# Batch 1's softmax divided behind v, the float64 shift on another engine, pinned first conversions and halved k loads in a fused attention and mixer kernel

## The chip, the cores and the metric

The kernel runs on one core of a Trainium2 chip. A core has a matrix engine (TensorE, PE in the rows, with its weight loads as PEld), a vector engine (VectorE, DVE), an engine for activation functions (ScalarE, ACT), a general one (GpSimd, POOL), an engine whose sequencer starts transfers here (SyncE, SP), and 16 DMA engines. Each engine runs its instructions in one fixed order, and semaphores make one wait for another. Data lie in SBUF (128 partitions), sums of matmuls in the banks of PSUM. The metric is the device time of one execution in microseconds; before the change it is 533.94 us, the median of three runs (531.52 to 535.51).

## What is computed

Four batches of 576 positions, 8 heads of 64. Heads 0 to 3 look at the last 32 positions, heads 4 to 7 at every 32nd. The weights of the mixers come as float64.

```python
scores = np.where(mask, q @ k.T / np.sqrt(64), -1e9)
attn = np.exp(scores - scores.max(-1))
x = (attn / (attn.sum(-1) + 1e-9)) @ v            # heads side by side: [4, 576, 512]
h = np.maximum(x @ w_in, 0)                       # first mixer
u, v = h[..., :512], h[..., 512:]
vn = (v - v.mean(-1)) / np.sqrt(v.var(-1) + 1e-6)
x = (u * (w_spatial @ vn + b_spatial)) @ w_out
th = x @ w_theta                                  # second mixer
u = x + w_tok_r @ (x * cos(th)) + w_tok_i @ (x * sin(th))
out = u + np.maximum(u @ w_ch, 0)
```

## The kernel before

All products of the mixers are made from float16 halves: a number is split into a high and a low half, and three matmuls (high by high, low by high, high by low) are added in PSUM. A weight arrives as raw float64 in a staging tile (`x2f`, `zf`, `xT`, before these are needed for themselves) and is put together as float32 by `from_f64` (line 200): ScalarE scales the upper words (L207), VectorE shifts the lower words (L208) and joins them (L209, L210); `part` then makes the halves, the high one on ScalarE (L119), the low one on GpSimd (L215). There are 15 such conversions: four of w_in, two each of w_out, w_theta and w_ch, five of the token weights.

Attention runs over 11 units a batch (`units`, line 274); a unit is two blocks of 96 or 128 queries with 128 keys for two heads, four softmax tiles. Batches 0 and 1 use `attention32` (line 420) in float32, batches 2 and 3 `attention` (line 488) in float16 halves. A unit of `attention32` goes through TensorE's mask matmuls and scores (`scores32`, L398, L403), VectorE's maximum (L410), ScalarE's four exponentials with their sums (L420) and two small instructions (L418, L354), VectorE's reciprocal and division (L357, L358), TensorE's four transposes (L460), ScalarE's copy of them (L461), the product with v (L435), and the eviction into xT, the high half by ScalarE (L370), the low one by VectorE (L371). In batch 1, transposes and products share one PSUM bank, `av`, of which there is one; scores have another, `sc`. k comes with zeros beside it (`padded`), so that one matmul of 128 partitions sees one head.

A batch of the mixers is `main_v` (v, its normalisation `rstd` and vn), `main_mid` (u and sp chunks, then x, then th with the sines of z, stored transposed by DMA into `zf`) and `main_end` (y over the token weights, then c and the store). Their evictions have a raised priority (`hv`, `ha`, `hg`).

The program is written in one order and the scheduler puts each engine's instructions in order by priorities and readiness as it estimates them. `ATT_AT` says at which count of matmul columns the steps of the next batch's attention are written into the mixers, `CONV_SP` to `CONV_CH` the same for the conversions, `WIN_AT` after which steps of batch 0's attention the four w_in conversions are written. So batch 0's attention comes first with w_in's conversions in it, then batch 0's v, then `main_mid(0)` with batch 1's attention in it; what is left of that is drained, then `main_v(1)`, then `main_end(0)` with batch 2's attention.

Of the kernel before, what the change touches and what calls it, by code (L numbers as in the profile page):

```python
# [15 lines left out]
I64 = mybir.dt.int64  # L16
AF = mybir.ActivationFunctionType
# [17 lines left out]
E_WAY = ('aaaadaaadaa', 'aaaaaaaaaaa')  # L35
# [19 lines left out]
WIN_AT = (0, 0, 0, 0, 1, 0, 1, 0)  # L55
# [9 lines left out]
def kernel(  # L65
# [31 lines left out]
    NZ = 2 * S // P  # L97

# [35 lines left out]
    nc.gpsimd.tensor_copy(identb, ident)  # L134
    halfpi = const.tile([P, 1], F32, name="halfpi")
# [64 lines left out]
    def from_f64(stg, x, n):  # L200
# [6 lines left out]
        nc.scalar.activation(hi.bitcast(F32), hi.bitcast(F32), AF.Copy, scale=F64_SHIFT)  # L207
        nc.vector.tensor_scalar(xi, lo, 29, None, op0=ALU.logical_shift_right)  # L208
# [11 lines left out]
    def prep_w(dst, src, c, i, late=True):  # L220
        stg, x = stage(raw2)
        n = c.stop - c.start
        nc.sync.dma_start(pair(stg, n), src[i * P:(i + 2) * P, c].rearrange("(a p) n -> p a n", p=P))
        x = pair(from_f64(stg, x, 2 * n), n)
# [62 lines left out]
    def prep_qk(b, hp, j, tiles):  # L287
        local = hp < 2
        nk = S + STRIDE if local else S
        if j == 0:  # L290
            qT = att_p.tile([P, 2, S], F16, tag="qT", name="qT", bufs=2)
            kT = att_p.tile([P, 2, 2, S + STRIDE], F16, tag="kT", name="kT", bufs=2)
# [21 lines left out]
    def load32(b, hp):  # L314
# [3 lines left out]
        kv = att_p.tile([P, 2, S + STRIDE], F32, tag="kT", name="k32", bufs=2)  # L318
# [10 lines left out]
        vv = att_p.tile([P, 6, 2, 64], F32, tag="vT", name="v32", bufs=2)  # L329
        nc.sync.dma_start(vv[:, 0:nb], vl_d[b, hp] if local else vs_d[b, hp - 2])  # L330
# [8 lines left out]
    def softmax_exp(u, sc, sm, st):  # L339
# [83 lines left out]
    def attention32(b):  # L423
# [5 lines left out]
        for s in range(NU + 2):  # L429
# [483 lines left out]
```

## Time and profile before

| | us |
|---|---|
| median of 3 runs | 533.94 |
| the profiled execution | 533.31 |
| its span in the trace | 531.5 |
| TensorE busy in the span | 481.9 |
| VectorE busy | 357.2 |
| ScalarE busy | 309.8 |
| GpSimd busy | 92.8 |

In the profile a row of a timeline is start in us, duration in us, engine, line, operation, tiles (out<-in), shapes and count, and in brackets how long the engine was idle ahead of it and what released it. A table by stretches gives the stretch and its length, then for each of PE, PEld, DVE, ACT and POOL the busy time and the count, TensorE's granted clock as a share of 2.4 GHz, the DMA engines' busy share and GB/s. A group by line gives its count, then busy us and mean ns, then the idle time ahead with what ended it. A wait row gives the instruction, what it waited for, the total in us, the times and the longest. The stretches used are: 0 to 56.56 batch 0's attention (in it most of v's first matmuls), to 63.70 the rest of its v, to 155.21 u, sp, x and th of batch 0 with batch 1's attention, to 169.85 batch 1's v, to 203.18 batch 0's y, and then all the rest.

### The profile page before, as it was taken

To read this page: it belongs to the slowest core of one execution; us is meant where nothing else is said; L and a number is where in the kernel's file an instruction comes from. 1 tells how busy PE (TensorE), PEld (TensorE's weight loads), DVE (VectorE), ACT (ScalarE), POOL (GpSimd) and SP (SyncE) were. 2 spreads that over 40 slices of the span, in tenths; PEclk is the share of its full clock that TensorE was granted. 3 is DMA by queue.
4 is the path that set the end of the run, shared out by engine and by line. 5 is a ranking of instruction groups with operands and counts; after the bars stand their busy time and mean duration, and the time that the engine had idled before them with its cause. 6 is when DMAs were issued, how large, how long until landed. Compare 5 with 4: busy or idle time off the path is not lost. (4 is left out here: it accounts for less than half of the span.)

```text
span 531.5 us, 10195 instructions
## 1 busy us (share of the span) xinstructions
PE 481.9 (91%) x4019; PEld 362.3 (68%) x4019; DVE 357.2 (67%) x721; ACT 309.8 (58%) x751; POOL 92.8 (17%) x58
## 2 busy tenths in 40 slices
PE   5577976889798979999899998999999999998996
PEld 5564554667564757777675886777757777776774
DVE  1789789899959988888649877875289221226512
ACT  2787767678799246786676456865593111238202
POOL 0021115463300261001000400000001400100110
PEclk9789989999999989999999999999999999999999
DMA  8875652844339404666419035532054011002702
GB/s 273 316 242 176 211 197 77 267 123 172 122 72 190 157 5 119 189 131 154 123 37 166 1 58 138 153 53 41 1 110 69 1 46 46 1 1 51 129 2 89
DMA packets 75700, 59.88 MB, mean 113 GB/s; under 512 B 59778, under 2 KB 60802, under 8 KB 75652
## 3 DMA queue, kind: packets, MB, share of 16 engines
q1 hardware_dynamic: 75652, 59.23, 41.7%
q8 instruction: 31, 0.51, 0.4%
q14 instruction: 17, 0.14, 0.1%
HBM read 40.08 MB, written 4.72 MB: 84 GB/s over the span
## 5 line engine op out<-in xcount | busy, mean ns | idle before, releaser
L532 PE MATMUL y<-wtok,zf 128*128 128x288 f16 x864 | 108.5, 288 | 1.5 <-DMA zf<-vn 1.5
L532 PEld LDWEIGHTS <-zf 128*128 128x128 f16 x864 | 84.6, 99 | 24.5 <-DMA zf<-vn 1.8
L532 PE MATMUL sp<-wsp,vn 128*128 128x288 f16 x384 | 50.5, 286 | 3.8 <-ACT vn L108 1.9
L532 PE MATMUL c<-x2h,wch 128*128 128x288 f16 x384 | 48.8, 286 | 2.4 <-ACT o L108 2.4
L532 PE MATMUL u<-xT,win 128*128 128x288 f16 x384 | 50.5, 290 | 0.0
L532 PEld LDWEIGHTS <-vn 128*128 128x128 f16 x416 | 40.3, 98 | 14.3 <-ACT vn L108 2.1
L532 PE MATMUL th<-x2h,wth 128*128 128x288 f16 x384 | 49.7, 290 | 0.0
L532 PE MATMUL x<-zf,wout 128*128 128x288 f16 x384 | 49.2, 286 | 0.0
L108 POOL TENSOR_TENSOR x2h<-x2f,x2h 128x576 f16<-128x576 f32 x20 | 27.0, 1349 | 109.9 <-DVE x2h L108 47.6
L532 PEld LDWEIGHTS <-wch 128*128 128x128 f16 x384 | 37.3, 98 | 12.1 <-issue 3.0
L592 PE MATMUL v<-win,xT 128*128 128x512 f16 x192 | 43.5, 379 | 1.6 <-ACT xT L370 1.4
L532 PEld LDWEIGHTS <-wth 128*128 128x128 f16 x384 | 37.7, 99 | 10.3 <-issue 0.5
L532 PEld LDWEIGHTS <-win 128*128 128x128 f16 x384 | 37.9, 99 | 9.7
L532 PEld LDWEIGHTS <-wout 128*128 128x128 f16 x384 | 37.1, 98 | 9.4
L348 ACT ACTIVATE sm<-sm,st 96x128 f32<-96x128 f32 (+1 forms) x88 | 34.2, 390 | 8.1 <-DVE st L344 8.1
L592 PEld LDWEIGHTS <-xT 128*128 128x128 f16 x192 | 18.3, 98 | 23.5 <-ACT xT L370 2.3
L108 POOL TENSOR_TENSOR zf<-u,zf 128x576 f16<-128x576 f32 x8 | 14.0, 1746 | 112.1 <-ACT zf L108 112.1
L108 ACT ACTIVATE x2h<-x2f 128x576 f16<-128x576 f32 x24 | 16.4, 685 | 28.8 <-DVE x2f L108 28.4
L358 DVE TENSOR_TENSOR sm<-sm,st 96x512 f32<-96x512 f32 (+1 forms) x33 | 29.6, 897 | 0.9
L108 DVE SCALAR_TENSOR_TENSOR x2f<-y,x2f 128x576 f32<-128x576 f32 x16 | 12.0, 753 | 26.5 <-PE y L532 26.4
L108 DVE TENSOR_TENSOR ta<-ta,x2f 128x1152 f32<-128x1152 f32 x16 | 21.6, 1353 | 9.7 <-ACT ta L108 9.7
L108 ACT ACTIVATE o<-c 128x576 f32<-128x576 f32 (+1 forms) x17 | 10.3, 613 | 29.9 <-PE c L532 29.7
(132 smaller groups left out, 861.5 us busy)
## 6 DMA issues: line engine op xcount, KB each, us to landing
qs<-in_qd_dram SPq DMA_DIRECT2D x16, 288.0 KB, 2.8
out_dram<-o SPq DMA_DIRECT2D x15, 288.0 KB, 2.1
ks<-in_kl_dram SPq DMA_DIRECT2D x8, 304.0 KB, 3.2
k<-in_kzs_dram SPq DMA_DIRECT2D x4, 576.0 KB, 6.1
ks<-in_ks_dram SPq DMA_DIRECT2D x8, 288.0 KB, 3.0
x2f<-in_w_in_dram SPq DMA_DIRECT2D x2, 1024.0 KB, 5.2
zf<-in_w_in_dram SPq DMA_DIRECT2D x2, 1024.0 KB, 9.9
xT<-in_w_ch_dram SPq DMA_DIRECT2D x2, 1024.0 KB, 6.2
```

The source lines that it names most:

```text
L108: return f(*args, **kwargs)
L348: nc.scalar.activation(sm[0:R, n, :], sm[0:R, n, :], AF.Exp, bias=st[0:R, 1, n:n + 1], scale=-1.0, accum_out=st[0:R, 2, n:n + 1])
L358: N[eng].tensor_tensor(sm[0:R], sm[0:R], st[0:R, 3, :].unsqueeze(2).broadcast_to([R, 4, P]), ALU.mult)
L532: nc.tensor.matmul(ps, lhs, rhs, **kw)
L592: nc.tensor.matmul(ps, xh[:, xe, c, i * P:(i + 1) * P], win[:, we, c, DM:2 * DM], start=(c == 0 and n == 0), stop=(c == NC - 1 and n == 2))
```

## The change

1. The first two w_in loads are issued together, and their conversions keep the order of the program (`win_ahead`, `pin`); `WIN_AT` is moved.
2. The shift of the lower words in `from_f64` goes from VectorE to ScalarE, which reads one byte of each and scales it.
3. k of batches 0 and 1 is loaded in two halves of 64 partitions, without zeros, into two constant tiles `kts` zeroed once by VectorE; the first loads are issued by ScalarE's sequencer, and the mask comes in two halves. Batches 2 and 3 use the same two tiles for their k.
4. Batch 1 has a function of its own. Its mask is added by VectorE, which finds the maximum in the same instruction (the form of batches 2 and 3). v carries columns of ones, so its product brings the sums of the exponentials along; it is made with the probabilities as stationary operand, is divided as it leaves PSUM, and is transposed after that. The pipeline has one step more.

```diff
-WIN_AT = (0, 0, 0, 0, 1, 0, 1, 0)
+WIN_AT = (0, 1, 0, 0, 0, 1, 0, 1)
...
+    kts = [const.tile([P, 2, S + STRIDE], F32, name=f"kt{i}") for i in range(2)]
+    for t in kts:
+        nc.vector.memset(t[0:64, 1, :], 0.0)
+        nc.vector.memset(t[64:P, 0, :], 0.0)
...
-        nc.scalar.activation(hi.bitcast(F32), hi.bitcast(F32), AF.Copy, scale=F64_SHIFT)
-        nc.vector.tensor_scalar(xi, lo, 29, None, op0=ALU.logical_shift_right)
+        order = tc.keep_in_program_order if pin else lambda ins: ins
+        order(nc.scalar.activation(hi.bitcast(F32), hi.bitcast(F32), AF.Copy, scale=F64_SHIFT))
+
+        top = stg.bitcast(U8)[:, 0:8 * n].rearrange("p (n w) -> p n w", w=8)[:, :, 3]
+        order(nc.scalar.activation(xi, top, AF.Copy, bias=1.0 / 64 - 0.5, scale=1.0 / 32))
...
+    def win_ahead(half):
+        c = slice(half * DM, (half + 1) * DM)
+        loaded = {}
+
+        def load():
+            for i in range(0, NC, 2):
+                loaded[i] = load_w(w_in, c, i)
+
+        return [load] + [lambda i=i: prep_w(win, w_in, c, i, False, loaded[i]) for i in range(0, NC, 2)]
...
-            nc.sync.dma_start(kv[..., k0:k1], ksrc[..., k0:k1])
-            if first and i == 0:
-                nc.sync.dma_start(mask, mask_d)
-                nc.scalar.activation(maskb, mask, AF.Copy)
...
+            for j in range(2):
+                h = slice(64 * j, 64 * j + 64)
+                (nc.scalar if first else nc.sync).dma_start(kv[h, j, k0:k1], ksrc[h, j, k0:k1])
...
+            vv = att_p.tile([P, 6, VW], F32, tag="vT", name="v32", bufs=2)
+            nc.gpsimd.memset(vv[:, 0:nb, 0:VW:VW - 1], 1.0)
+            nc.sync.dma_start(vv[:, 0:nb, 1:VW - 1], vsrc.rearrange("p n j d -> p n (j d)"))
...
+    def attention1(b):
...
+            if s >= 3:
+                xn, rows = xs.pop(s - 3)
+                for i, hp, blk, r0, R, o, t0 in pv_blocks(s - 3):
+                    nc.tensor.transpose(xt[:, o:o + R], xn[0:R, i, :], ident[0:R, 0:R])
+            if 2 <= s < NU + 2:
+                sm, pT, st, xn = un.pop(s - 2)
+                for i, hp, blk, r0, R, o, t0 in pv_blocks(s - 2):
+                    for j in range(2):
+                        c = slice(j * (VW // 2), (j + 1) * (VW // 2))
+                        nc.tensor.matmul(pv[0:R, i, c], pT[:, 2 * i + j, r0:r0 + R], tabs[hp][2][:, blk, c],
+                                         start=True, stop=True)
+                ri = st[0:R, 3, :].rearrange("p (i j) -> p i j", i=2)
+                nc.scalar.activation(ri, pv[0:R, :, 0:VW:VW - 1], AF.Copy, bias=1e-9 / XS, scale=1.0 / XS)
+                nc.vector.reciprocal(st[0:R, 3, :], st[0:R, 3, :])
+                nc.vector.tensor_tensor(xn[0:R].rearrange("p i (j d) -> p i j d", j=2),
+                                        pv[0:R, :, 1:VW - 1].rearrange("p i (j d) -> p i j d", j=2),
+                                        ri.unsqueeze(3).broadcast_to([R, 2, 2, 64]), ALU.mult)
+                xs[s - 2] = xn, R
+            if s >= 3:
+                x_evac(xT[b % 2], spans_of(s - 3), xt)
...
+                softmax_exp(s, [sc[:, n, :] for n in range(4)], sm, st, False)
```

In the changed kernel the lines are numbered anew: L216 and L219 are the scale and the shift of a conversion, L456 batch 0's exponentials and L384 those of the other batches, L492 and L406 batch 0's copy of transposes and the eviction's high half, L407 its low half; in batch 1 L547 are the transposes of the exponentials, L548 their copy, L516 the product with v, L519 to L521 the division, L510 the transposes behind it.

ScalarE early in batch 0's attention, before: `at` are scores, `smx` exponentials, `x2f` the first part of w_in.

```order
L418 ACTIVATE st_134<-st_134 96x4
L420 ACTIVATE smx_124,st_134<-at_125,st_134 96x128 x4
L418 ACTIVATE st_149<-st_149 96x4
L207 ACTIVATE x2f_99<-x2f_99 128x1024
L420 ACTIVATE smx_141,st_149<-at_142,st_149 96x128 x4
L354 ACTIVATE st_134<-st_134 96x4
L418 ACTIVATE st_180<-st_180 96x4
```

The first conversion stands ahead of the second unit's exponentials. The same conversion in the changed kernel:

```order
L492 ACTIVATE smx_214<-sc_263 128x4x96
L216 ACTIVATE x2f_105<-x2f_105 128x1024
L219 ACTIVATE x2h_106<-x2f_105 128x1024
L406 ACTIVATE xT0_101<-av_275 128x192
L492 ACTIVATE smx_247<-sc_306 128x4x96
L456 ACTIVATE smx_319,st_327<-at_320,st_327 128x128 x3
L492 ACTIVATE smx_288<-sc_337 128x4x96
L216 ACTIVATE zf_104<-zf_104 128x1024
L121 ACTIVATE win_87<-x2h_106 128x2x512
```

It stood at row 6 of ScalarE's order and stands at row 34 now, behind the exponentials of the first units, and a shift follows it.

ScalarE where batch 0's th ends and batch 1's v begins, before: `ta` are the sines and cosines, `vn` here the halves of z, `xT1` batch 1's xT.

```order
L108 ACTIVATE vn_97<-ta1_1475 128x1152
L108 ACTIVATE ta3_1554<-ta3_1554 128x576
L370 ACTIVATE xT1_96<-av_1522 128x18x14
L108 ACTIVATE vn_97<-ta2_1511 128x1152
L108 ACTIVATE ta3_1554<-ta3_1554,halfpi_79 128x576
L108 ACTIVATE ta3_1554<-ta3_1554 128x576
L119 ACTIVATE kT_1849<-ks_1852 128x608
L119 ACTIVATE qT_1848<-qs_1924 128x576
L307 ACTIVATE vT_1999<-vs_1895 128x768
L108 ACTIVATE vn_97<-ta3_1554 128x1152
```

Batch 1's last eviction (L370) stands among the sines. In the changed kernel, at the same sines:

```order
L519 ACTIVATE st_1330<-av_1467 126x4
L216 ACTIVATE xT0_101<-xT0_101 128x1024
L110 ACTIVATE vn_103<-ta2_1546 128x1152
L110 ACTIVATE ta3_1594<-ta3_1594,halfpi_85 128x576
L110 ACTIVATE ta3_1594<-ta3_1594 128x576
L406 ACTIVATE xT1_102<-av_1467 128x18x4
L384 ACT_TABLE_LOAD
L384 ACTIVATE sm_1882,st_1883<-sm_1882,st_1883 96x128
L110 ACTIVATE vn_103<-ta3_1594 128x1152
L406 ACTIVATE xT1_102<-av_1467 128x18x4
```

The evictions here are those of the ninth unit of eleven; a shift, a table load and an exponential of batch 2 stand between.

TensorE where batch 1's last product with v stands, before:

```order
L532 LDWEIGHTS wth_85
L532 MATMUL th2_1486<-x2h_100,wth_85 128x288
L435 MATMUL av_1522<-pT32_1367,v32_1207 64x126 x4
L532 LDWEIGHTS wth_85
L532 MATMUL th3_1529<-x2h_100,wth_85 128x288
```

It stood in batch 0's th stage. In the changed kernel the last unit's transposes, products and transposes behind the division stand in batch 1's v stage, among scores of batch 2 (L560):

```order
L560 LDWEIGHTS qT_1774
L560 MATMUL sc_1948<-kt0_79,qT_1774 96x128
L547 MATMUL av_1481<-ident_70,sm_1399 128x128 x4
L510 MATMUL av_1557<-ident_70,pT32_1329 128x126 x2
L516 MATMUL av_1557<-v32_1235,pT32_1400 126x65 x4
L510 MATMUL av_1605<-ident_70,pT32_1400 128x126 x2
```

Behind it come one group of scores more and the last 39 of batch 1's 60 v matmuls; 21 stand ahead.

## Rows read from the trace of the kernel before

**Rows 1.** Table by stretches of the span: busy time of each engine.
```profile
0.00:18.80 18.80, 7.92 (x57) 7.21 (x58) 4.85 (x11) 6.38 (x23) 0.99 (x7) 0.89 0.88 306
18.80:39.81 21.01, 17.01 (x143) 14.76 (x143) 18.49 (x35) 18.10 (x72) 4.25 (x2) 0.85 0.74 250
39.81:56.56 16.75, 13.18 (x97) 7.19 (x95) 15.10 (x24) 12.81 (x42) 4.47 (x2) 1.00 0.57 188
...
63.70:155.21 91.51, 76.42 (x624) 58.47 (x624) 80.17 (x114) 68.13 (x178) 33.81 (x14) 0.96 0.47 154
155.21:169.85 14.64, 13.16 (x70) 5.63 (x68) 13.38 (x22) 14.61 (x24) 0.00 (x0) 1.00 0.83 146
169.85:203.18 33.33, 29.99 (x253) 23.69 (x253) 30.81 (x70) 16.01 (x36) 13.42 (x7) 0.95 0.31 88
203.18:531.50 328.32, 317.07 (x2751) 242.34 (x2749) 189.29 (x443) 168.13 (x373) 35.89 (x26) 1.00 0.34 77
```

**Rows 2.** Timeline, all engines: where the longest wait of TensorE ends.
```profile
16.23 1.14 ACT L207 ACTIVATE x2f<-x2f 128x1024 f32<-128x1024 f32 x1 [5.74 <-DMA x2f<-in_w_in_dram]
16.23 0.69 DVE L208 TENSOR_SCALAR x2h<-x2f 128x1024 int32<-128x1024 int32 x1 [5.98 <-DMA x2f<-in_w_in_dram]
...
18.80 0.58 PE L398 MATMUL at<-maskb,identb 128*96 128x256 bf16 x2 [5.92 <-ACT smx L420]
```

**Rows 3.** TensorE's waits, 0 to 70 us.
```profile
PE at L403 <- DMA k<-in_kzl_dram: 2.3, 2, 1.3
```

**Rows 4.** TensorE's waits, 65.15 to 155.21 us.
```profile
PE av L460 <- DVE xT L371: 9.5, 4, 3.5
...
PE av L460 <- DVE sm L358: 1.7, 3, 0.7
```

**Rows 5.** Groups by line, 65.15 to 155.21 us.
```profile
L358 DVE TENSOR_TENSOR sm<-sm,st 96x512 f32<-96x512 f32 (+1 forms) x10 | 13.8, 1378 | 0.2
...
L410 DVE TENSOR_REDUCE st<-sc 96x4 f32<-96x512 f32 (+1 forms) x10 | 6.7, 674 | 0.5 <-PE sc L403 0.4
...
L207 ACT ACTIVATE zf<-zf 128x1024 f32<-128x1024 f32 (+1 forms) x4 | 4.9, 1224 | 0.8 <-DMA zf<-in_w_tr_dram 0.5 <-DMA zf<-in_w_out_dram 0.3
...
L371 DVE TENSOR_TENSOR xT<-av,xT 128x192 f16<-128x192 f32 (+2 forms) x11 | 3.8, 342 | 0.5 <-ACT xT L370 0.4
L398 PE MATMUL sc<-maskb,identb 128*128 128x512 bf16 (+2 forms) x10 | 3.6, 376 | 0.0
```

**Rows 6.** Timeline, GpSimd and VectorE near 87 us.
```profile
85.72 4.32 POOL L108 TENSOR_TENSOR vn<-vr,vn 128x1024 f16<-128x1024 f32 x1 [1.25 <-ACT vn L108]
...
87.98 2.61 DVE L358 TENSOR_TENSOR sm<-sm,st 96x512 f32<-96x512 f32 x1
```

**Rows 7.** Timeline of TensorE: the v stages of batch 0 and batch 1.
```profile
55.69 0.60 PE L592 MATMUL v<-win,xT 128*128 128x512 f16 x2 [0.48 <-ACT xT L370]
...
162.94 6.22 PE L592 MATMUL v<-win,xT 128*128 128x512 f16 x28 [0.23 <-DVE xT L371]
```

**Rows 8.** Timeline of ScalarE: exponentials of the first unit.
```profile
7.88 0.36 ACT L420 ACTIVATE smx<-at,st 96x128 f32<-96x128 f32 x1
8.14 0.19 ACT L420 ACTIVATION_READ_ACCUMULATOR smx<-at,st 96x1 f32 x1
8.23 0.35 ACT L420 ACTIVATE smx<-at,st 96x128 f32<-96x128 f32 x1
```

**Rows 9.** Timeline of VectorE: the mask form that batches 2 and 3 use.
```profile
165.33 0.28 DVE L344 CUSTOM_DVE_ANT_0 sm<-sc,mask 96x128 f32<-96x128 f32 x1
...
165.54 0.28 DVE L344 CUSTOM_DVE_ANT_0 sm<-sc,mask 96x128 f32<-96x128 f32 x1
```

**Rows 10.** Timeline of TensorE in the y stage of batch 0.
```profile
187.95 4.57 PE L532 MATMUL y<-wtok,zf 128*128 128x288 f16 x36
195.86 1.01 PE L473 MATMUL sc<-kT,qT 128*96 128x128 f16 x8 [3.34 <-DVE st L344]
196.66 5.73 PE L532 MATMUL y<-wtok,zf 128*128 128x288 f16 x36
```

More of the change, by code (lines that the diff above doesn't have):

```diff
@@ L16 @@
 I64 = mybir.dt.int64
+U8 = mybir.dt.uint8
 AF = mybir.ActivationFunctionType
@@ L34 @@
 V_ORDER = (0, 1, 2)
-E_WAY = ('aaaadaaadaa', 'aaaaaaaaaaa')
+E_WAY = 'aaaadaaadaa'
 E_WHI = 'aa'
@@ L97 @@
     NZ = 2 * S // P
+    VW = 2 * 64 + 2
     class Ahead:
@@ L218, in pair, with load_w, prep_w @@
         return ap[:, 0:2 * n].rearrange("p (a n) -> p a n", a=2)
-    def prep_w(dst, src, c, i, late=True):
+    def load_w(src, c, i):
         stg, x = stage(raw2)
+        nc.sync.dma_start(pair(stg, c.stop - c.start), src[i * P:(i + 2) * P, c].rearrange("(a p) n -> p a n", p=P))
+        return stg, x
+    def prep_w(dst, src, c, i, late=True, loaded=None):
+        stg, x = loaded or load_w(src, c, i)
         n = c.stop - c.start
-        nc.sync.dma_start(pair(stg, n), src[i * P:(i + 2) * P, c].rearrange("(a p) n -> p a n", p=P))
-        x = pair(from_f64(stg, x, 2 * n), n)
+        x = pair(from_f64(stg, x, 2 * n, loaded is not None), n)
         part(dst[:, 0, i:i + 2, c], dst[:, 1, i:i + 2, c], x, late)
@@ L457, in attention32 @@
                 softmax_div("v", sm, st, R, XS)
-                pt = pa4("sc" if b == 0 else "av")
+                pt = pa4("sc")
+                for n in range(4):
+                    nc.tensor.transpose(pt[:, n, 0:R], sm[0:R, n, :], ident[0:R, 0:R])
+                nc.scalar.activation(pT[:, :, 0:R], pt[:, :, 0:R], AF.Copy)
+            yield
+    def attention1(b):
+        tabs = {0: load32(b, 0)}
+        yield
+        tabs[1] = load32(b, 1)
+        un, xs = {}, {}
+        for s in range(NU + 3):
+            if s >= 2:
+                av = pa("av")
+                pv = av[:, 0:2 * VW].rearrange("p (i n) -> p i n", i=2)
+                xt = av[:, 2 * VW:512]
+            if s >= 3:
[18 more added lines that the diff above has]
+                x_evac(xT[b % 2], spans_of(s - 3), xt)
+            if s in (5, 8):
+                tabs[s // 3 + 1] = load32(b, s // 3 + 1)
+            if s < NU:
+                sm = att_p.tile([P, 4, P], F32, tag="sm", name="sm", bufs=2)
+                pT = att_p.tile([P, 4, P], F32, tag="pT", name="pT32", bufs=2)
+                st = att_p.tile([P, 4, 4], F32, tag="st", name="st", bufs=4)
+                xn = pT[:, 0:2]
+                sc = pa4("sc")
+                R = LQ if units[s][0][0] < 2 else P
+                for n, (hp, j, blk) in enumerate(blocks_of(s)):
+                    o = LQ * blk if hp < 2 else SOFF[blk]
+                    nc.tensor.matmul(sc[0:R, n, :], tabs[hp][0][:, o:o + R], tabs[hp][1][:, j, o:o + P],
+                                     start=True, stop=True)
+                softmax_exp(s, [sc[:, n, :] for n in range(4)], sm, st, False)
+                un[s] = (sm, pT, st, xn)
+            if 1 <= s <= NU:
+                sm, pT, st, xn = un[s - 1]
+                R = LQ if units[s - 1][0][0] < 2 else P
+                pt = pa4("av")
@@ L774, in timed @@
             conv.append((due - lead - gap * (len(parts) - 1 - i), f))
-    for k, f in enumerate(list(win_parts(1)) + list(win_parts(0))):
+    for f in win_ahead(1) + list(win_parts(0)):
         conv.append((-1e9, f))
@@ L782 @@
     timed(sq_parts(wch, w_ch), *CONV_CH)
-    atts = [(attention32 if b < N32 else attention)(b) for b in range(B)]
+    atts = [attention0(0), attention1(1)] + [attention(b) for b in range(N32, B)]
     att = {"b": 1, "n": 0}
```

42 lines of the change are left out of this document (22 added, 20 removed).

## The prediction

> **What bounds the kernel now.** The profiled execution took 533.31 us over a span of 531.5 us, so 1.8 us lie outside the span; the median of the three runs shown, 533.94 us, is 0.6 us above it. I read first the table by stretches [rows 1]: after 203.18 us TensorE is busy in 317.07 of 328.32 us, and the change has almost no part there. It idles before: 10.88 us to 18.80, 4.00 and 3.57 us in the next two stretches, 15.09 us from 63.70 to 155.21, 1.48 us in batch 1's v stage, 3.34 us in the y stage behind it. Then I read what it waits for, stretch by stretch.
>
> At the start one wait is the bulk: 5.92 us that end at 18.80 [rows 2]. ScalarE stood at the first w_in conversion (L207) until its transfer landed at 16.23, and behind it, in ScalarE's order, stood the exponentials of a softmax unit whose scores buffer TensorE needed. VectorE's L208 stood at the same transfer. Two waits on k's transfers make 2.3 us [rows 3]; a head pair's k with its zeros is 128 x 2 x 608 floats, 608 KB, and the DMA engines are 88% busy there [rows 1].
>
> From 63.70 to 155.21 VectorE is busy in 80.17 of 91.51 us, ScalarE in 68.13 [rows 1]. TensorE's largest wait is for batch 1's attention: 9.5 us in four waits of a transpose (L460) for the eviction L371, because both use the one buffer `av`, and 1.7 us for the division L358 [rows 4]. L358 takes 1378 ns on average here [rows 5]; the one at 87.98 took 2.61 [rows 6].
>
> **The start.** The two w_in loads are issued together and their conversions keep program order; on ScalarE the first conversion now stands behind the exponentials of the first units. The 5.92 us wait has nothing left to wait for. The 1.14 us of L207 [rows 2] is ScalarE's price of a shift of the same size: four in w_in's conversions, 4.6 us more for ScalarE, 4 x 0.69 us less for VectorE. What is late next is ScalarE. It is busy 6.38 + 18.10 + 12.81 = 37.3 us up to 56.56 [rows 1], where the last v of batch 0 waits for its xT eviction at 55.69 [rows 7]. With the shifts it has 42 us of work; it starts exponentials at 7.88 [rows 8], perhaps 1 us earlier. If all but 2 to 4 us of idle go, the last eviction falls at 47 to 51 instead of 55.7. I take 8 us of gain; bounds are 5 us (the wait less what the shifts cost ScalarE beyond its idle time) and 11.
>
> k without zeros is half of 608 KB; at 306 GB/s [rows 1] that is 1 us a head pair, of which the first counts, in the 2.3 us of [rows 3], and is in the 8. The four memsets lie on VectorE before its first reduction, when it has nothing to do. Against the halves speaks the Trainium skill, DMA: Bandwidth & Descriptors, section Rules for kernel authors: two transfers to disjoint partition halves serialise, so one over all partitions is the better. By that page splitting gives nothing; the gain of a pair is then the missing bytes alone, which is what the sum above uses, and the trace of before, which has no such pair, shows neither.
>
> **63.70 to 155.21.** By engine, from [rows 5]. VectorE loses ten L358 (13.8 us), ten reductions L410 (6.7) and the shifts (nine here, about 0.7 each by [rows 2], 6). It gains four mask-and-maximum instructions a unit, 0.21 us apart as L344's starts show [rows 9], 0.84 x 10 = 8.4; and a multiply that reads PSUM, priced by L371, which also has one PSUM operand and took 342 ns on average with GpSimd running [rows 5]: 3.5. Net 26.5 - 11.9 = 14.6: 80.2 falls to 65.6. ScalarE gains nine shifts at 1.1 to 1.2 (L207 there 1.22 [rows 5]): 10.5. It loses the accumulator reads and one small instruction a unit; exponentials with a read start 0.35 apart [rows 8], four of them 1.4; without it no row shows the pitch. Bounds are 0.35 and the 0.26 after which the read itself starts; I take 0.31, so 1.25 and, with a small one gone, 0.3 less a unit: 3. ScalarE goes from 68.1 to 75.6. TensorE loses ten mask matmuls (3.6 [rows 5]) and gets two transposes a unit back, about 2.5: 76.4 falls to 75.
>
> So the bound moves: VectorE had 88% of the stretch, and now TensorE and ScalarE both have 75 us. The 9.5 us for L371 shrink, since VectorE is free sooner, but the `av` chain is longer: PV matmul, ScalarE's L519, reciprocal, multiply, ScalarE's L406, VectorE's L407, and only then the next transposes, two ScalarE instructions where there was one. I leave 6 us of waiting: 81 us instead of 91.5, a gain of 10. Bounds: 13 if ScalarE's queue costs half of that, 3 if each of 10 units still waits 1.3 us.
>
> The Trainium skill, SBUF — State Buffer, section Who interferes with whom, says that a VectorE instruction with two SBUF inputs contends with a GpSimd one that reads SBUF, and one with a single SBUF input does not. The trace agrees: 2.61 us for L358 at 87.98 inside a GpSimd instruction of 4.32 us that began at 85.72 [rows 6]. By the page the multiply that replaces it never pays that; by the row of L371 it costs the same 3.5 us, so the sum stands.
>
> **Batch 1's v stage and y.** This is what the change costs. Here ScalarE is busy in 14.61 of 14.64 us [rows 1] with the sines of z. Batch 1's attention has one pipeline step more, and the order of the changed kernel puts its last `av` chain (transposes L547, then L510, L516, L510) into this stage, behind 21 of the 60 v matmuls: its ScalarE instructions stand behind the sines, one shift, a table load and exponentials of batch 2. Worked from the order with durations of rows: the eviction L406 of the third last unit comes about 12.5 us after th ends, the transposes 1 us later, their eviction at 16.5 behind four exponentials and two casts, the division at 18, the last eviction at 20.5. Then 39 matmuls of v remain; as 28 took 6.22 us [rows 7], they take 8: y starts at 28.5 instead of 14.64, some 13.5 us later. What comes back: the scores of batch 2 that stood in y are done by then (at most three groups, of 1.01 us for the slowest [rows 10]: 2 us), the 3.34 us wait at 195.86 goes, and with it the slow matmuls behind it, 5.73 us for as many as took 4.57 before it [rows 10], 1.2. But a wait as long costs clock: the granted clock was 0.85 in the stretch behind the 5.92 us wait [rows 1], a mix of the levels 2.4 and 1.2 GHz, and the y rows put its price at 1.2; I take 1.5. 13.5 - 6.5 + 1.5 = 8.5 us lost. Bounds: 3, if the chain slips into gaps, and 13, if nothing returns.
>
> After 203 us the order repeats that of before with k in the constant tiles: 0, plus or minus 1.
>
> **The sum.** 533.3 - 8 - 10 + 8.5 = 523.8; counted from the median of the runs, 524.4. I say 524.
>
> **The rivals.**
> 1. *As forecast*, 518 to 529.
> 2. *ScalarE eats the middle's gain.* It has 75.6 us of work, every unit passes through it four times, and its order is fixed. For it: the evictions of u, x2 and z stand in the same queue. Against it: VectorE sheds 14.6 us. Then the middle gains 3, the start 7, the tail costs 8.5: 531 to 532.
> 3. *The tail hides.* The chain's late instructions find ScalarE free, the tail costs 2 and the y wait goes: 533.3 - 8 - 10 + 2, with the clock: 517 down to 512. Against it: ScalarE's 14.61 of 14.64.
> 4. *Slower.* One mechanism: TensorE's order is fixed, so nothing of v or y can pass the `av` chain, and y cannot start before it. If the chain ends not 20.5 but 36 us or more behind th (a sine group of z ahead of each of its four ScalarE steps, 4 us each), y starts 29 us later, the tail costs 24 (29 - 6.5 + 1.5) or more, and the whole is 539 to 543. That is the point from which it decides: 24 = 8 + 10 + 6.
> 5. *The change doesn't do what it says*: the pinned conversion still stands ahead of some exponentials when its transfer, now queued with the second, lands later. The wait stays at about 5 us; 528 to 530.
>
> **How the numbers follow.** Chances: 0.48 forecast, 0.22 rival 2, 0.15 rival 3, 0.08 rival 4, 0.07 rival 5. About 1% (5.3 us) is what a measurement of this kernel can tell from no change: faster is under 528.6, slower over 539.3. Under 528.6 lie nearly all of the forecast (0.46), rival 3, a third of rival 5 and a little of rival 2: 0.68. Slower: 0.07, most of rival 4. The rest, 0.25. The range goes from 513 (rival 3 but for its best) to 533 (rival 2 with its spread); rival 4 and the ends are left out.
>
> **What would show it.** No wait of TensorE over 2 us before 30 us; batch 0's last eviction near 48; u of batch 0 starting near 57 instead of 65. Between there and th's end some 81 us, VectorE below 75% busy, ScalarE above 90%, waits of transposes for L407 below 6 us, the L521 rows near 0.35 us whether or not GpSimd runs. From th's end to y some 28 us with waits at L547 for L407 and at L516 or L510 for ScalarE. Wrong would be: a middle over 86 us (rival 2), a v stage under 20 us (rival 3) or over 44 (rival 4), or a wait for L219 or L216 at the start (rival 5).

## The result and the profile after

The changed kernel takes 528.21 us (median of four runs, 527.33 to 529.65), the kernel before, run beside it, 534.01 (four runs, 531.52 to 535.51). The ratio is 0.9894 with an interval of 0.985 to 0.9938: about 5.8 us faster, where 10 were forecast. The profiled execution took 527.33 us over a span of 525.5, 6.0 us less than the span before. The table by stretches of the changed kernel, cut where [rows 1] are cut (start, middle, batch 1's v, y, rest; columns as there):

```profile
0.00:60.93 60.93, 48.85 (x326) 35.84 (x326) 39.84 (x79) 42.90 (x139) 9.68 (x13) 0.89 0.68 211
60.93:141.02 80.09, 73.40 (x620) 60.10 (x620) 69.06 (x170) 70.47 (x132) 29.49 (x16) 1.00 0.53 173
141.02:172.64 31.62, 21.73 (x103) 10.23 (x100) 27.56 (x65) 27.83 (x61) 0.00 (x0) 0.78 0.78 154
172.64:200.06 27.42, 27.42 (x237) 21.84 (x237) 22.74 (x38) 11.14 (x15) 12.26 (x7) 1.00 0.21 72
200.06:525.50 325.44, 316.72 (x2751) 242.01 (x2749) 185.36 (x438) 165.97 (x369) 35.91 (x26) 1.00 0.34 74
```

| us | before | after | difference | forecast |
|---|---|---|---|---|
| start | 63.70 | 60.93 | -2.8 | -8 |
| middle: batch 0's u to th | 91.51 | 80.09 | -11.4 | -10 |
| batch 1's v | 14.64 | 31.62 | +17.0 | +13.5 |
| batch 0's y | 33.33 | 27.42 | -5.9 | -5 (-6.5 and +1.5 for the clock) |
| rest | 328.32 | 325.44 | -2.9 | 0 |

The middle is what was forecast, the start is worth a third of its forecast, the tail (batch 1's v and batch 0's y together) costs 2.6 us more than forecast, and the rest gives 2.9 that nobody counted on.

**The start.** TensorE's timeline, of after and then of before:

```profile
16.68 0.38 PE L434 MATMUL at<-maskb,identb 128*128 128x256 bf16 x2
19.95 1.95 PE L439 MATMUL at<-kt,q 128*128 128x128 f32 x8 [2.88 <-DMA kt<-in_kzs_dram]
...
36.70 0.59 PE L434 MATMUL at<-maskb,identb 128*128 128x256 bf16 x2 [1.81 <-ACT smx L456]
```

```profile
24.02 0.38 PE L398 MATMUL at<-maskb,identb 128*128 128x256 bf16 x2
```

The mask matmuls of the third head pair stand at 24.02 in before and at 16.68 now, 7.3 us ahead. Then TensorE waits 2.88 us for that pair's k, which SP issues at 11.32, behind the two w_in transfers of 1 MB each (5.92 and 7.32) and batch 2's v of 384 KB (7.75). That k was as late before. SP's issues in before, and a transfer with its size and the time to its landing:

```profile
6.42 0.56 SPq L223 DMA_DIRECT2D zf<-in_w_in_dram  x1
...
11.03 0.56 SPq L325 DMA_DIRECT2D k<-in_kzs_dram  x1
```

```profile
k<-in_kzs_dram SPq DMA_DIRECT2D x1, 576.0 KB, 10.0
```

The w_in transfers left together in before too (5.71 and 6.42), so by time of issue part 1 changes nothing there. The k landed at about 21, and TensorE wanted it only at 24.24 (17.06 in after, at the end of the mask matmuls): the wait of 5.92 us had hidden it. ScalarE stands behind the same k, in after:

```profile
22.58 0.49 ACT L492 ACTIVATE smx<-sc 128x384 f32<-128x384 f32 x1 [4.14 <-PE sc L491]
```

The granted clock is 0.76 from 16 to 37 us, a mix of 1.2 and 2.4 GHz, where it was 1.00 ahead of the wait, and ScalarE's conversions now stand among the later units (L216 at 26.31 and 30.34, L219 at 27.36 and 32.55); the wait at 36.70 ends behind them. The first matmul of u starts at 62.22 instead of 65.15.

**The middle.** TensorE's waits from 62 to 141 us, then groups by line there:

```profile
PE av L547 <- DVE xT L407: 4.3, 6, 1.3
```

```profile
L220 DVE SCALAR_TENSOR_TENSOR x2h<-x2f,x2h 128x1024 int32<-128x1024 int32 x2 | 5.8, 2921 | 0.0
...
L521 DVE TENSOR_TENSOR pT<-av,st 96x256 f32<-96x256 f32 (+2 forms) x9 | 3.8, 417 | 0.1
```

The 9.5 us of [rows 4] are 4.3 us. TensorE idles 6.7 us (80.09 less 73.40), where 6 were left for it. Of batch 1's eleven evictions L371 of [rows 5] eight are left in this stretch (L407 in the groups by line): part of the stage's gain is work that now comes in the next one.

**Batch 1's v stage.** th ends at 141.02. Timeline of the chain that was in question, from ScalarE and TensorE:

```profile
151.49 0.21 ACT L406 ACTIVATE xT<-av 128x72 f16<-128x72 f32 x1
...
156.14 0.96 PE L547 MATMUL av<-ident,sm 128*128 128x128 f32 x4
...
161.88 0.37 ACT L406 ACTIVATE xT<-av 128x252 f16<-128x252 f32 x1
...
162.48 1.06 PE L679 MATMUL v<-win,xT 128*128 128x512 f16 x2
```

```profile
164.47 7.48 PE L679 MATMUL v<-win,xT 128*128 128x512 f16 x28
```

The last eviction stands 20.9 us behind th's end (20.5 forecast), and one group of batch 2's scores stands between it and v. The 28 matmuls that took 6.22 us in [rows 7] take 7.48: the stage has a granted clock of 0.78.

### The profile page after: what moved, and what is told of

It is laid out like the page before. It is cut to its first block, busy times and chain, and to the rows that moved or that the text cites. A ratio compares the mean times of both kernels' runs of the same rounds, so it can differ in the third digit from the quotient of the medians.

```text
span 525.5 us, 10260 instructions
## 1 busy us (share of the span) xinstructions
PE 488.1 (93%) x4028; PEld 370.0 (70%) x4028; DVE 344.6 (66%) x787; ACT 318.3 (61%) x712; POOL 87.3 (17%) x62
## 5 line engine op out<-in xcount | busy, mean ns | idle before, releaser
L619 PE MATMUL y<-wtok,zf 128*128 128x288 f16 x864 | 107.0, 286 | 1.5 <-DMA zf<-vn 1.5
L384 ACT ACTIVATE sm<-sm,st 96x128 f32<-96x128 f32 (+1 forms) x132 | 49.3, 392 | 10.8 <-DVE st L380 9.5
L679 PE MATMUL v<-win,xT 128*128 128x512 f16 x192 | 47.6, 401 | 4.8 <-ACT xT L406 4.3
L619 PE MATMUL u<-xT,win 128*128 128x288 f16 x384 | 49.3, 286 | 0.0
L619 PE MATMUL th<-x2h,wth 128*128 128x288 f16 x384 | 48.2, 286 | 0.0
L380 DVE CUSTOM_DVE_ANT_0 sm<-sc,mask 96x128 f32<-96x128 f32 (+1 forms) x132 | 31.5, 279 | 1.5 <-PE sc L538 1.4
L110 POOL TENSOR_TENSOR zf<-u,zf 128x576 f16<-128x576 f32 x8 | 11.4, 1431 | 112.0 <-ACT zf L110 112.0
L110 ACT ACTIVATE o<-c 128x576 f32<-128x576 f32 (+1 forms) x17 | 10.3, 612 | 30.3 <-PE c L619 30.0
L110 DVE TENSOR_TENSOR ta<-ta,x2f 128x1152 f32<-128x1152 f32 x16 | 21.6, 1353 | 10.3 <-ACT ta L110 10.3
```

The lines of the kernel that those rows point to most:

```text
L110: return f(*args, **kwargs)
L380: nc.vector.tensor_tensor_reduce(out=sm[0:R, n, :], in0=sc[n][0:R], in1=mask[0:R, mask_of(hp, blk), :], op0=ALU.add, op1=ALU.min, scale=-0 ...
L619: nc.tensor.matmul(ps, lhs, rhs, **kw)
L679: nc.tensor.matmul(ps, xh[:, xe, c, i * P:(i + 1) * P], win[:, we, c, DM:2 * DM], start=(c == 0 and n == 0), stop=(c == NC - 1 and n == 2))
```

## The experiments

Stages are named as in the table above; "u to v of batch 2" is the stretch from the first u matmul of batch 0 to the first v matmul of batch 2, two whole batches of mixer, in which the order can shift work between stages. It takes 210.5 us before (65.15 to 275.63) and 208.3 after (62.22 to 270.51). All ratios are against the kernel before, run on the same chip; a letter in an expectation stands for what the text beside it says.

### The four parts, each undone

The first conversions as before (part 1 undone):

```diff
-WIN_AT = (0, 1, 0, 0, 0, 1, 0, 1)
+WIN_AT = (0, 0, 0, 0, 1, 0, 1, 0)
...
-    for f in win_ahead(1) + list(win_parts(0)):
+    for f in list(win_parts(1)) + list(win_parts(0)):
```

> The changed kernel with part 1 undone: the w_in loads and conversions are written one after the other as before and not pinned. The changed kernel for comparison: batch 0's u begins at 62.2 us, the middle (end of batch 0's v to end of th) is 80.1, batch 1's v stage 31.6, the whole 528.2. Theory A (the pin is what removed the wait at the first conversion): the wait of 5 to 6 us near 18 us is back, u begins at 65 or later, the whole 531 to 534. Rival B (the start is bound by the transfers, whatever the order of the conversions): no more than 1 us changes, 527 to 529.

Measured: 533.33 us (ten runs), ratio 0.999 (0.9956 to 1.0023). The wait is back, and longer, in TensorE's timeline:

```profile
17.52 0.58 PE L434 MATMUL at<-maskb,identb 128*96 128x128 bf16 x4 [8.32 <-ACT smx L456]
```

So part 1 does take away the wait of [rows 2], and the whole needs it: 5.1 us. Yet u starts at 63.54, only 1.3 us later than in after. The stretch up to u in before, in after and here:

```profile
0.00:65.15 65.15, 46.70 (x342) 33.59 (x342) 44.88 (x80) 44.07 (x146) 9.71 (x11) 0.92 0.72 242
```

```profile
0.00:62.22 62.22, 50.14 (x339) 37.12 (x340) 40.86 (x80) 44.17 (x141) 9.68 (x13) 0.89 0.67 206
```

```profile
0.00:63.54 63.54, 45.10 (x338) 32.23 (x339) 43.83 (x83) 45.80 (x144) 9.70 (x13) 0.95 0.64 203
```

TensorE idles 18.4 us in before and here, and 12.1 in after: the pin does take 6.4 us of idle time away. But in after TensorE is busy 5.0 us longer than here for as many matmuls, at a granted clock of 0.89 against 0.95.

The shift back on VectorE, under the same pin (part 2 undone):

```diff
-        order(nc.scalar.activation(xi, top, AF.Copy, bias=1.0 / 64 - 0.5, scale=1.0 / 32))
+        order(nc.vector.tensor_scalar(xi, lo, 29, None, op0=ALU.logical_shift_right))
```

> The changed kernel with part 2 undone: VectorE shifts the lower words again. Theory A (ScalarE's conversions ate the start's gain): ScalarE has 4.4 us less before batch 0's u, which begins 2 to 3 us sooner, at 59 to 60; the middle has VectorE at 75 of 80 us and grows by 2 to 3. The whole 526 to 529. Rival B (the third head pair's k, behind the w_in loads, ate it): u begins at 61.5 to 62.5, and the whole is 528 to 531.

Measured: 542.27 us (four runs), ratio 1.0164 (1.0124 to 1.0204): 14 us slower than after, which neither side expected. u starts at 69.22; the wait for the third pair's k is 5.0 us (TensorE's waits up to 69 us), and u to v of batch 2 takes 216.5:

```profile
PE at L439 <- DMA kt<-in_kzs_dram: 5.0, 1, 5.0
```

Two runs further down take this apart.

k with its zeros and in one transfer again (part 3 undone):

```diff
-        kv = kts[hp % 2]
+        kv = att_p.tile([P, 2, S + STRIDE], F32, tag="kT", name="k32", bufs=2)
...
-            for j in range(2):
-                h = slice(64 * j, 64 * j + 64)
-                (nc.scalar if first else nc.sync).dma_start(kv[h, j, k0:k1], ksrc[h, j, k0:k1])
+            nc.sync.dma_start(kv[..., k0:k1], ksrc[..., k0:k1])
```

> The changed kernel with part 3 undone: k with its zeros, one transfer of 128 partitions, all issued by SyncE's queue, no constant tiles (the mask still comes in halves). Rival B (the transfers bind the start): the wait for the third head pair's k grows from 2.9 to 4 or 5 us and the first scores come later; u begins at 64 to 65, the whole 530 to 532. If bytes of k do not bind: u at 62 to 62.5 and the whole 527.5 to 529.

Measured: 529.91 us (nine runs), ratio 0.9942 (0.9917 to 0.9967). In TensorE's timeline the same wait is longer by 1.5 us, and u starts 1.8 us later, at 64.03:

```profile
21.75 1.62 PE L433 MATMUL at<-k,q 128*128 128x128 f32 x6 [4.42 <-DMA k<-in_kzs_dram]
```

By the medians part 3 is worth 1.7 us; the intervals of the two ratios overlap, so the runs can't tell that from nothing, and only the rows show a difference. The edit also puts the first loads back on SP and takes away the constant tiles, so the rows speak for part 3 as a whole. The Trainium skill, DMA: Bandwidth & Descriptors, section Rules for kernel authors, would rather have one transfer over all partitions than two to disjoint halves. Here the two carry half the bytes, and by these rows they come out ahead; what the splitting costs by itself was not measured.

Batch 1 by the function of before (part 4 undone):

```diff
-    atts = [attention0(0), attention1(1)] + [attention(b) for b in range(N32, B)]
+    atts = [attention32(0), attention32(1)] + [attention(b) for b in range(N32, B)]
```

> The changed kernel with part 4 undone: batch 1's attention as before, on the halved k. Theory A (part 4 gives in the middle and takes in the v stage, by its one step more): start as in the changed kernel (u at 62.2), middle 84 to 88 instead of 80.1 since L358 and L410 are back on VectorE, v stage 15 to 20 instead of 31.6, y 30 to 33; the whole 524 to 528. Rival (the v stage's loss comes from the scheduler's placing, not from the step): v stage stays at 25 or more, the whole 531 to 535.

Measured: 535.16 us (ten runs), ratio 1.0019 (0.9981 to 1.0057). The middle is 83.25 us, near after's. The v stage (table by stretches, and its longest wait) is as long as in after, with the pipeline of before:

```profile
145.30:178.08 32.78, 19.66 (x105) 10.08 (x103) 25.40 (x49) 28.24 (x57) 1.28 (x1) 0.74 0.75 182
```

```profile
PE sc L503 <- ACT sm L450: 7.3, 1, 7.3
```

So the additional pipeline step, to which the prediction put the tail, is not needed for it. u to v of batch 2 takes 214.3 us, 6.0 more than in after: most of the 7.0 that undoing part 4 costs.

### The shift alone, and the shift back without the pin

The kernel before with part 2 and nothing else:

```diff
-        nc.vector.tensor_scalar(xi, lo, 29, None, op0=ALU.logical_shift_right)
+        top = stg.bitcast(U8)[:, 0:8 * n].rearrange("p (n w) -> p n w", w=8)[:, :, 3]
+        nc.scalar.activation(xi, top, AF.Copy, bias=1.0 / 64 - 0.5, scale=1.0 / 32)
```

> The kernel before with part 2 alone: the shift on ScalarE. Theory E (part 2 carries the change, since undoing it cost 14 us): the whole 526 to 530, with u of batch 0 at 62 to 65. Rival F (undoing it cost 14 us because the shift was then pinned on VectorE, and it is worth little by itself): 531 to 536, with the wait at the first conversion unchanged at 5 to 6 us, the middle shorter by 5 to 8, and as much lost again in batch 1's v stage, where the last chain has moved by the order.

Measured: 533.72 us (ten runs), ratio 0.9987 (0.9952 to 1.0023). The wait of the start stays (5.62 us, ending at 18.50). The table by stretches, u to th of batch 0, v of batch 1 and y:

```profile
66.02:146.12 80.10, 72.19 (x592) 56.00 (x591) 65.31 (x97) 69.36 (x176) 30.19 (x14) 0.98 0.50 170
146.12:171.57 25.45, 17.22 (x90) 7.97 (x88) 21.62 (x36) 23.12 (x40) 0.00 (x0) 0.80 0.75 156
171.57:200.67 29.10, 28.51 (x254) 22.86 (x253) 26.61 (x58) 14.66 (x29) 11.54 (x7) 1.00 0.24 76
```

One instruction of a conversion, moved to another engine, shortens this stretch by 10 us (90.1 before, from 65.15 to 155.21) and lengthens the v stage by 10.8. Batch 1's attention is as before here. So the shorter middle and the longer v stage go together: th is over sooner, and the last units of batch 1's attention, with what batch 2's puts between, come behind it.

After with the shift on VectorE, and without the pin on it:

```diff
-        order(nc.scalar.activation(xi, top, AF.Copy, bias=1.0 / 64 - 0.5, scale=1.0 / 32))
+        nc.vector.tensor_scalar(xi, lo, 29, None, op0=ALU.logical_shift_right)
```

> The changed kernel with the shift back on VectorE and, unlike in the run before, not pinned there. Theory F (the pin on VectorE made that run slow): u of batch 0 at 62 to 66 instead of 69, the whole 529 to 535. Theory E (VectorE's work itself): u at 68 or later, the whole 539 to 543.

Measured: 538.21 us (eight runs), ratio 1.0071 (1.0037 to 1.0105). Of the 14 us of the pinned one 4 were the pin's. Of the other 10, two lie ahead of u, which starts at 64.17 (62.22 in after), and nine between it and v of batch 2: that stretch by engine in before, after and this kernel, then with the shift alone and with part 4 undone.

```profile
65.15:275.63 210.48, 187.48 (x1604) 140.72 (x1603) 177.65 (x348) 148.46 (x366) 52.42 (x25) 0.98 0.49 136
```

```profile
62.22:270.51 208.29, 190.32 (x1616) 145.05 (x1615) 169.13 (x413) 156.95 (x332) 46.95 (x27) 0.97 0.52 140
```

```profile
64.17:281.58 217.41, 194.56 (x1617) 148.72 (x1615) 178.56 (x419) 143.55 (x317) 47.14 (x27) 0.95 0.47 129
```

```profile
66.02:274.66 208.64, 187.28 (x1604) 141.21 (x1603) 169.31 (x339) 159.03 (x379) 47.43 (x25) 0.97 0.51 142
```

```profile
63.50:277.75 214.25, 187.95 (x1604) 141.46 (x1603) 175.93 (x341) 162.80 (x382) 50.41 (x25) 0.95 0.48 136
```

With parts 1, 3 and 4 but not 2, VectorE is busy 178.56 us, as much as before (177.65). That total hides two changes. VectorE's busy time in this stretch by line, in us (batch 1's masks are those of L380 less the 10.28 us that batch 2's take in before):

| | before | this kernel | after |
|---|---|---|---|
| batch 1's division and maximum (L358, L410), then its masks and L521 | 20.5 | 14.8 | 15.0 |
| the shifts (L208, then L219) | 8.5 | 12.1 | none |
| the joins (L209, L210, then L220, L221) | 30.3 | 31.8 | 34.2 |

Batch 1's new function does take 5.8 us off VectorE, but here the conversions take 5.1 us more, for the same eleven shifts and 22 joins. Taking the shifts away saves 8.5 us in after, of which the longer joins eat 3.9. The totals swing as much where VectorE's instructions are nearly the same: the two kernels with the shift moved and batch 1's old function have 339 and 341 of them, and are busy 169.31 and 175.93 us. What makes the same join longer is shown in the last section. Undone one by one the parts cost 5.1, 10 to 14, 1.7 and 7.0 us, some 24 to 28 together, and together they gain 5.8: they don't add.

### The start: k of the third pair ahead of the second w_in transfer

```diff
-        nc.sync.dma_start(pair(stg, c.stop - c.start), src[i * P:(i + 2) * P, c].rearrange("(a p) n -> p a n", p=P))
+        ld = nc.sync.dma_start(pair(stg, c.stop - c.start), src[i * P:(i + 2) * P, c].rearrange("(a p) n -> p a n", p=P))
+        if pin:
+            tc.keep_in_program_order(ld)
```

The second load is written and pinned behind that k's, and batch 2's first loads (k, q and v of its first head pair) are pinned too.

> The changed kernel, but the second w_in load is issued behind the third head pair's k, and batch 2's first q, k and v loads keep the order of the program (before they were issued among the first). Theory B (the start waits for the third head pair's k, 2.9 us in the changed kernel, because 2.4 MB stand in front of it): that wait is under 1 us, batch 0's u begins at 58 to 60 instead of 62.2, the whole 524 to 526. Rival A (ScalarE binds the start): the wait goes but u begins at 61.5 to 62.5, the whole 527 to 529.

Measured: 536.81 us (six runs), ratio 1.0067 (1.0024 to 1.011). The wait for k is gone (0.48 us, for q), and u starts at 59.36, 2.9 us ahead of after:

```profile
17.63 1.23 PE L445 MATMUL at<-kt,q 128*128 128x128 f32 x8 [0.48 <-DMA q<-in_qp_dram]
```

But batch 2's first loads come late as well, and in y TensorE waits for them (38.79 us instead of 27.42):

```profile
PE sc L566 <- DVE qT L332: 3.7, 1, 3.7
```

y still begins 3.4 us sooner than in after, at 169.19. So what stood ahead of that k, with the clock and the waits that follow from it, accounts for 2.9 of the 5.1 us by which u's start fell short (8 forecast, 2.9 measured); the other 2.2 are open. The edit takes both the second w_in transfer and batch 2's v from ahead of k and does not tell them apart. A late load without the second pin was not tried.

### The tail: batch 1's last steps ahead

In three kernels the last steps of batch 1's attention got a raised priority; the first also wrote the steps 3.6 apart, the second raised all of batch 1's, the third had the late loads of above besides the first's edit.

```diff
-        if next(atts[att["b"]], "end") == "end":
+        with tc.high_priority(400 if att["b"] == 1 and att["n"] >= 8 else 0):
+            done = next(atts[att["b"]], "end") == "end"
+        if done:
```

> The changed kernel, but batch 1's attention steps are written every 3.6 instead of 4.0 of the column clock, and its steps from the ninth on with a raised priority; so its last chain stands in th's stage on TensorE, ahead of all 60 v matmuls. In the changed kernel the middle, batch 1's v stage and y take 80.1 + 31.6 + 27.4 = 139.1 us, before 91.5 + 14.6 + 33.3 = 139.5. Theory C (the v stage's loss is the place of the last chain in the orders): v stage 14 to 18, y 27 to 29, middle 83 to 87; the sum 126 to 133, the whole 515 to 522. Rival D (the sum is bound by the work of VectorE and ScalarE, so that any place costs the same): the v stage shortens, the middle grows by as much, the sum stays at 138 to 140, the whole 527 to 530.

> As the run with the raised priority, but for all steps of batch 1's attention, at the old spacing of 4.0. Theory C: the attention ends earlier still; v stage 14 to 16; the mixers' evictions now stand behind it, so the middle is 84 to 90; the sum of middle, v stage and y 128 to 135, the whole 517 to 524. Rival D: sum 138 to 140, whole 527 to 530.

> The late loads and the raised priority together. Theories B and C: both gains add, u at 58 to 60, sum of middle, v stage and y 126 to 133, the whole 512 to 519. If either fails, its share is missing: 515 to 526.

Measured: 578.67, 584.79 and 582.69 us (four runs each; ratios 1.089, 1.0993 and 1.0946, each known to 0.005). The v stage falls to 11.9 us in the first, but the 0 in the edit moved all other steps too, ahead of everything, batches 2 and 3 among them. From y of batch 0 to the end that takes 417.9 us, after takes 352.9. TensorE's timeline shows what this does: the matmuls of attention stand one by one between those of the mixer.

```profile
206.34 0.30 PE L619 MATMUL c<-x2h,wch 128*128 128x288 f16 x1
206.57 0.23 PE L583 MATMUL av<-pT,vT 128*64 128x96 f16 x1
206.73 0.30 PE L619 MATMUL c<-x2h,wch 128*128 128x288 f16 x1
...
210.38 0.29 PE L619 MATMUL c<-x2h,wch 128*128 128x288 f16 x1
210.50 0.22 PE L560 MATMUL sc<-kt,qT 128*96 128x128 f16 x1
210.56 0.29 PE L619 MATMUL c<-x2h,wch 128*128 128x288 f16 x1
```

These runs say nothing on the tail's worth. The next edit gives the other steps no priority at all, and raises only the steps from the thirteenth on, by 200:

```diff
-ATT_AT = (None, (2.7, 4.0), (74.5, 4.4), (169.9, 4.6))
+ATT_AT = (None, (2.7, 3.6), (74.5, 4.4), (169.9, 4.6))
...
+        with tc.high_priority(200) if att["b"] == 1 and att["n"] >= 12 else nullcontext():
+            done = next(atts[att["b"]], "end") == "end"
```

> The run with the raised priority once more, but with it on the last steps of batch 1's attention alone; in that run the steps of batches 2 and 3 had got a raised priority too, which broke up everything behind y's start (y itself began at 161.5 us instead of 172.6). Theory C (the v stage's loss is the place of the last chain): v stage 12 to 15, y 27 to 29, middle 84 to 89, sum of the three 126 to 131 instead of 139.1, the rest at 325 to 329; the whole 516 to 521. Rival D (the sum is bound by the work of VectorE and ScalarE): y pays back what the v stage gained, the whole 526 to 530.

Measured: 528.96 us (eleven runs), ratio 0.9914 (0.9879 to 0.9948), the same as after; the profiled execution was its fastest, 525.7. The table by stretches (u to th, v, y) and TensorE's one large wait in y:

```profile
61.71:146.48 84.77, 76.64 (x623) 61.53 (x623) 70.64 (x178) 73.09 (x139) 31.08 (x16) 0.98 0.51 166
146.48:158.36 11.88, 11.88 (x63) 5.20 (x60) 10.86 (x11) 11.88 (x17) 0.00 (x0) 1.00 0.65 132
158.36:195.52 37.16, 30.52 (x263) 24.21 (x261) 34.41 (x79) 21.51 (x46) 13.29 (x7) 0.91 0.43 103
```

```profile
183.26 1.01 PE L560 MATMUL sc<-kt,qT 128*96 128x128 f16 x8 [6.64 <-DVE st L380]
```

The v stage has no wait left and gives back 19.7 us, yet the middle takes some 6 more (from u on), and y 9.7 more, because batch 2's first scores, which in after run in the gaps of the v stage, now stand in y, where VectorE is late. From u to c of batch 0 that is 133.8 us where after takes 137.8; from u to v of batch 2 1.3 us of these 4.0 are left. The last try wrote batch 2's steps later, so that y need not wait:

```diff
-ATT_AT = (None, (2.7, 3.6), (74.5, 4.4), (169.9, 4.6))
+ATT_AT = (None, (2.7, 3.6), (81.0, 4.2), (169.9, 4.6))
```

> The run with the raised priority on the last steps, and batch 2's attention written later (from 81.0 instead of 74.5 of the column clock, every 4.2 instead of 4.4), so that its second group of scores stands behind VectorE's normalisation of batch 1's v; in that run TensorE waited 6.64 us for it in y. Theory G (the wait is a matter of place): it is under 1.5 us, v stage 12, y 29 to 32, the sum of middle, v stage and y 126 to 130 instead of 133.8; the whole 2 to 8 us under that run's, 518 to 526. Rival D (VectorE's work is the bound): the wait comes back behind another instruction, the sum stays at 133 to 136, the whole 527 to 531.

Measured: 527.41 us (six runs), ratio 0.9881 (0.9834 to 0.9927), within its interval the same as after. The table by stretches, y and batch 1's u to th, and in the latter TensorE's longest wait:

```profile
159.87:189.96 30.09, 27.53 (x235) 22.09 (x234) 26.98 (x50) 16.08 (x26) 13.28 (x7) 1.00 0.43 114
...
206.39:271.05 64.66, 59.09 (x558) 45.71 (x556) 45.69 (x128) 45.07 (x118) 4.21 (x3) 0.95 0.48 126
```

```profile
PE av L583 <- DVE xT L407: 3.2, 1, 3.2
```

TensorE's wait for batch 2's scores in y falls from 6.6 to 2.6 us (under 1.5 expected), and u to c of batch 0 takes 128.2 us, inside the 126 to 130 of theory G; but the whole is as rival D had it. Batch 1's u begins at 206.39, 7.3 us ahead of after, and its u to th takes 64.66 us instead of 56.78: all given back. From u to v of batch 2 the kernels with the shift on ScalarE and batch 1's new function take 207.0 (this edit's forerunner), 208.3 (after), 209.3 (this one), 209.4 (part 3 undone) and 210.8 (part 1 undone), for quite different orders in between; with the late loads it is 221.2, with batch 2's loads behind. The shift alone comes to 208.6 without the new function, and before to 210.5. What holds them there is open: no engine is full (TensorE is busy 190.32 of after's 208.29 us, VectorE 169.13).

## Why the prediction was right or wrong

**Right: the direction, the range and the middle.** 528.21 lies in 513 to 533, at the upper edge of the 518 to 529 named for the forecast itself, and by 0.4 us under the 528.6 from which it was to count as faster. That is in part luck: the start and the tail came out 7.8 us worse than forecast and the middle and the rest 4.3 better, 2.9 of these by something not foreseen. The middle came to 80.09 us where 81 was forecast, with TensorE busy 73.40 (75), VectorE 69.06 (65.6), ScalarE 70.47 (75.6) and 6.7 us of waiting (6): rival 2 is out. Most prices of the operations held: L219 took 1.11 to 1.28 us (1.1 to 1.2), half-size ones aside. The division L521 took 0.417 us a unit where 0.35 was said, with GpSimd running or not, and ten units of masks (L380, with the reads of their accumulator) kept VectorE busy 10.0 us where four times the 0.21 us of [rows 9] made 8.4.

One term is missing: the sum for VectorE left the joins of the conversions as they were. They take 29.4 us in the middle (L220 14.6, L221 14.8), and 23.6 before (L209 12.8, L210 10.8). The prediction freed the division from GpSimd and did not ask what GpSimd would hold up in its place. Two signs did not come: VectorE was to be below 75% busy and ScalarE above 90%, and they are at 86% and 88%. The first went against the prediction's own sum, which has 65.6 of 81 us, 81%. And the middle is not a gain by itself: from u to v of batch 2 after is 2.2 us shorter than before.

**Wrong: the start, "I take 8 us of gain".** It was 2.8 us, below the lower bound of 5. The wait of 5.92 us did go, and TensorE stood 7.3 us ahead at 16.68. The step that failed is "If all but 2 to 4 us of idle go": ScalarE was idle for 9.0 us between its first exponentials and the last eviction, 4.14 of them in one wait that goes back to the third pair's k. That stretch of after, by engine:

```profile
8.35:52.23 43.88, 33.91 (x254) 26.05 (x253) 29.53 (x54) 34.85 (x126) 6.19 (x4) 0.84 0.70 220
```

The prediction named ScalarE as late next and did not ask whether that k, in before already behind the w_in transfers, would be there 7.3 us sooner. It cost TensorE 2.88 us, and behind it came a clock of 0.76 and conversions that now stand among later units. The first exponentials start at 8.35, and not 1 us ahead of the 7.88 of [rows 8]. The last eviction came at 52.23 (55.25 before; 47 to 51 forecast). Taking that k ahead gives u at 59.36; by that the bound of 5 would have held (65.15 less 59.36 is 5.8). "No wait of TensorE over 2 us before 30 us" was the sign that showed it. Rival 5 named 528 to 530, where the time nearly lies, but its mechanism is out: the wait at the first conversion is gone, and the one that took its place is for a load of k, not for L216 or L219.

**Half wrong: the tail, 8.5 us.** It cost 11.1 (17.0 less 5.9), inside 3 to 13. The chain was timed well, 20.9 us against 20.5. The mis-sized term is the 8 us for the last 39 matmuls: they took 10.2 (162.48 to 172.64) at a low clock, and a group of scores stood ahead of them. The clock was priced at 1.5 us and put into y, where it is 1.00. The cause was wrong too: not the additional pipeline step (undone, the stage takes 32.78 us) but where the order puts the last units once th ends sooner: the shift alone, with the pipeline of before, lengthens the stage by 10.8 of the 17.0 us. What the additional step adds to that was not measured. Rivals 3 and 4 are out as they were stated (31.62 us lies between 20 and 44).

**Not foreseen: -2.9 us in the rest.** TensorE's wait for batch 2's evictions there is 1.4 us in one wait, 2.6 in two before; c of batch 0 is 1.5 us shorter (200.06 to 213.73, before 203.18 to 218.35). What batch 2's attention did in the v stage it need not do later. That fits the last two runs, in which the v stage was shortened and the time came back behind it; that the two are the same 2.9 us was not shown.

Over the whole: the start gave 5.2 us less than forecast, the tail took 2.6 more, the middle gave 1.4 more and the rest 2.9, so 6.0 in place of 9.5 in the span.

## What to carry to other kernels

When a wait at the start goes, look for the next one that it had hidden: a small load behind two large ones was late all along, and nothing had asked for it in time. A stage that gets shorter hands its unfinished work to the next one, so follow a gain until both pipelines have passed, over whole batches, before it is counted. Parts that each seem needed when undone need not add up; time them together and by pairs. Busy time contains stalls, so compare an engine's instructions line by line before you say which change relieved it.

## What was not expected of the hardware

**Contention moves to the next instruction.** L358 stalled with GpSimd in [rows 6]; it is gone, and now L220 does. VectorE, and GpSimd at the same time:

```profile
76.19 1.22 DVE L220 SCALAR_TENSOR_TENSOR x2h<-zf,x2h 128x1024 int32<-128x1024 int32 x1
...
80.33 2.77 DVE L220 SCALAR_TENSOR_TENSOR x2h<-x2f,x2h 128x1024 int32<-128x1024 int32 x1
```

```profile
79.88 2.13 POOL L226 TENSOR_TENSOR wout<-x2h,wout 128x1024 f16<-128x1024 f32 x1 [4.90 <-ACT wout L121]
```

The same instruction takes 1.22 us with GpSimd idle and 2.77 beside it; the one at 80.33 ends 1.1 us after GpSimd's does. In the middle six of the eighteen joins start while a GpSimd instruction runs; each ends 0.6 to 1.2 us behind it, and these six are the long ones (1.50 to 3.07 us). In before two are long, 2.09 and 2.43 us. The Trainium skill, SBUF — State Buffer, section Who interferes with whom, says that an instruction of VectorE with two SBUF inputs contends with a GpSimd one that reads SBUF. The trace agrees, here and in L521, which has one SBUF input and never stalls; but the stall did not go with the instruction that had it: batch 1's division and maximum (nine divisions now, ten before) became 6.7 us cheaper in the middle and the joins 5.8 us dearer.

**Matmuls of 64 and 128 columns in turn are dear.** In the kernel with the raised priorities (rows at 206.34 above) a c matmul and an `av` product of tile 128*64 in turn take 0.39 us a pair; a c matmul and a score of tile 128*96 take 0.18 (210.38 to 210.56). In groups by line the 264 products took 10.3 us in after and 61.0 there:

```profile
L583 PE MATMUL av<-pT,vT 128*64 128x96 f16 (+2 forms) x264 | 10.3, 214 | 1.4 <-DVE xT L407 1.4
```

```profile
L583 PE MATMUL av<-pT,vT 128*64 128x96 f16 (+2 forms) x264 | 61.0, 233 | 0.0
```

An estimate from these, if all 264 stand one by one: 0.39 less a c matmul in a run (0.127) and a product in a group (0.039) is 0.22 us a pair, 59 us for 264, most of the 65 that this kernel lost behind 161 us. That the change of tile is the cause was not tried apart.
